# Attention with bucket masks and a mixture-of-experts step: one PSUM bank for the attention products, kd on GpSimd, most of R on VectorE, another order

## The chip, the cores and the metric

The kernel runs on one core of a Trainium2 chip. Its engines run side by side, each with its own queue of instructions, which it takes in order: TensorE (PE in the profile, its weight loads PEld), VectorE (DVE), ScalarE (ACT), GpSimd (POOL), and SyncE (SP), whose queue here issues nearly all DMAs. Semaphores tie them together. The metric is the device time of one execution in microseconds.

## The reference, cut to what matters

There are 4 batches of 8 heads, 768 tokens and 64 columns a head: 32 heads in all.

```python
q_bucket, k_bucket = hash_of(q, proj), hash_of(k, proj)      # 6 sign bits each
mask = q_bucket[:, :, :, None] == k_bucket[:, :, None, :]
scores = scale * np.matmul(q, k.transpose(0, 1, 3, 2))
scores = np.where(mask, scores, -1000000000.0)
scores = scores - np.max(scores, axis=-1, keepdims=True)
attn = np.exp(scores)
attn = attn / (np.sum(attn, axis=-1, keepdims=True) + 1e-09)
return np.matmul(attn, v)
```

A row without any key in its bucket has all its scores at the same large negative number, so its result is the mean of all values. The heads' results, side by side, are 512 columns wide per token. In each batch a gate then scores the 768 tokens, the best 128 pass through an expert (512 to 1024 columns, ReLU, back to 512), and the expert's result, times a sigmoid of the score, is added to these tokens.

## The kernel before

**Precision.** float32 operands are split into a high and a low part, and products are summed from the parts. `A` holds the high parts of q and k in rows 32 to 95, the signs of the hash bits in rows 0 to 5, and in row 96 the row maxima; `Bt` the cross parts. The signs put the mask into the scores: each differing bit lowers a score by a large amount.

**Per head**, the steps are these.

- Preparation: `load_x` brings q and k, `split_xh` (ScalarE) and `split_xl` (VectorE, line 167) split them, and `place_a`, `place_signs`, `place_b` move the parts into `A` and `Bt` by DMAs on SP's queue. For each pair of heads `load_v`, `split_vh`, `split_vl` make `V`: 64 high columns, a column of ones (times 16), 64 low columns.
- Maxima: `k_diff` (line 241, VectorE) subtracts the second half of the keys from the first. For each of six query tiles, `max_unit` (line 251) makes two 384-column products in two of the three `mx` banks, `max_relu` (line 258, ScalarE) takes the relu of one and `max_red` (line 265, VectorE) adds the other and takes the maximum over the row, since max(a, b) = relu(a - b) + b. `max_fin` (line 272) rounds the six columns, and `max_row` moves them into row 96 of `A`.
- Scores: nine units of 512 columns. `st_unit` (lines 283 and 287) makes two matmuls for each piece of a unit in a bank of `pst`, `st_exp` (lines 300 and 302, ScalarE) takes the exponential into `P`, in float32.
- R: the high half of the bits of `P` is read as a bfloat16; `r_chunk` (line 313) subtracts it from `P` and writes the rest as a float16. There are six chunks of 128 keys a head; `pool_r` says which of them GpSimd makes (four and five by turns; three and two in the last two heads), VectorE makes the others.
- Products: `av` (lines 326 and 330) takes 36 pairs of key chunk and query tile in four parts of nine. For each pair, the high part of `P` times all 129 columns of `V`, and R times the first 65. The six query tiles' sums lie in two banks of PSUM, 129 columns each: 64, the sum of the weights, and 64 from the low columns.
- Evacuation: `evac` (line 337, ScalarE) copies both banks to SBUF, `join` (line 345, GpSimd; VectorE in the last head) adds the two groups of 64 columns, `unmatched` (line 350) finds the rows whose sum is zero, `recip` and `recip2` (lines 357 and 363) make 1 / (sum + 1e-9), `norm` (line 371) multiplies into `x`, the batch's result, and `fix` (line 379) puts the mean of the values in the rows found. The means come from `load_vt` (v transposed, a load of its own), `sum_v` (line 213, ScalarE), `mean_v` (line 219, PE) and `mean_evac` (line 227, ScalarE).
- `score` (line 391, VectorE) makes the gate's scores from `x`.

**Per batch** `choose` writes `x` to the output on SP's queue, sends the scores to every partition, ranks the tokens on VectorE and gathers the chosen ones; `expert` does the rest. The experts' weights are split by `load_w` (line 415, GpSimd) in the first heads.

**The order** is written out by hand: each step is given a time in units, of which a head has nine, from the table `T` and `AVS`; all steps are emitted in the order of these times, and each engine runs its own in that order. The units count from `s0 = 9 * h`, the first unit of the head's scores; `b = s0 - 14` is the base of its maxima, `a0 = s0 + 6` that of its products. A pool with n buffers makes the tile that comes n later wait for the last reader.

PSUM's eight banks: three for `mx`, two for the scores, two for the products, one for the experts.

Of the kernel before, what the change touches and what calls it, by code (L numbers as in the profile page):

```python
# [11 lines left out]
F32 = mybir.dt.float32  # L12
# [3 lines left out]
I32 = mybir.dt.int32  # L16
# [18 lines left out]
PB = (3, 2)  # L35
XHB = 2
XLB = 2
AVS = ((0, 9, 1.34), (9, 18, 3.3), (18, 27, 5.62), (27, 36, 6.48))
# when an engine's part of the work is put in line, in units
T = dict(  # L40
    loadx=-34.22, hash=-5.69, hash2=2.32, sign=1.42, xh=-8.42, xl=-0.57, pa=-5.69, ps=0.26, loadv=-13.95,
    vh=-7.97, vl=-2.67, mean=4.21, loadt=-1.38, sumv=4.41, meane=0.56, exp=0.51, max=-0.24, kd=-1, mb=1.2,
    copy=0.71, red=2.2, fold=2.07, foldd=2.37, fin=0.81, unm=0.2, row=1.19, rp=2.6, rd=5.05, ev=0.72, rc=1.85,
    rc2=0.3, norm=0.95, fix=1.28, sc=2.97, scd=0.95, join=1.2, m1=-18.04, m2=-7.82, y1=1.01, sc3=0.3, f0=1.67,
    f1=1, f2=1.62, l0=0.84, l1=0.5, l2=1.32, l3=2.62, lw=-0.65, lw1=6.42, lw2=3.62, mo=0.38, ym=1, fold0=3.65,
# [26 lines left out]
def body(ctx, tc, qk, v, vt, pj, wg, w1, w2, cst, out):  # L72
# [131 lines left out]
    def load_vt(pr):  # L204
        t = sb.tile([P, S], F32, tag="V", name=f"VT{pr}", bufs=1)
        nc.sync.dma_start(t, vt[pr])
        st["VT", pr] = t

    def sum_v(pr):
        # the sums of the values over all tokens, one per partition  # L210
        sv = sb.tile([P, 1], F32, tag="sv", name=f"sv{pr}", bufs=2)
        jk = sb.tile([P, S], BF16, tag="jv", name=f"jv{pr}", bufs=1)
        nc.scalar.activation(jk, st["VT", pr], AF.Copy, accum_out=sv)
        st["sv", pr] = sv

    def mean_v(pr):
        # and in every partition
        mp = pmax.tile([P, 512], F32, tag="mx", name=f"mp{pr}")
        nc.tensor.matmul(
            mp[:, : 2 * D], st["sv", pr].broadcast_to([P, P]), ident, start=True, stop=True  # L220
        )
        st["mp", pr] = mp[:, : 2 * D].rearrange("p (h d) -> p h d", h=2)

    def mean_evac(pr):
        o = st["mp", pr]
        mv = sb.tile([P, 2, D], F32, tag="mv", name=f"mv{pr}", bufs=2)
        nc.scalar.activation(mv, o, AF.Copy, scale=1.0 / S)
        st["mv", pr] = mv

# [7 lines left out]
    # the row maxima: max(a, b) = relu(a - b) + b over the two halves of the keys  # L237
    def k_diff(h):
        a = A[h % NA]
        kd = sb.tile([96, 384], F32R, tag="kd", name=f"kd{h}", bufs=1)  # L240
        nc.vector.tensor_tensor(
# [28 lines left out]
    def max_fin(h):  # L270
        m = sb.tile([P, NC], F32R, tag="m", name=f"m{h}", bufs=2)
        nc.vector.tensor_copy(m, st["mA", h])
        st["m", h] = m
# [42 lines left out]
    def av(h, i0, i1):  # L316
        # (key chunk, query tile) pairs i0 to i1 of the 36
        vv, hh = V[h // 2 % NV], h % 2
        if i0 == 0:
            st["O", h] = pav.tile([P, 2, 512], F32, tag="av", name=f"av{h}")  # L320
        o = st["O", h][:, :, : 3 * (2 * D + 1)].rearrange("p e (t d) -> p e t d", t=3)
        for i in range(i0, i1):
            c, t = divmod(i, NC)
            e, j = divmod(t, 3)
            hi = hi_view(st["P", h, c // 2], c % 2)[:, t * P : (t + 1) * P]
            nc.tensor.matmul(  # L326
                o[:, e, j], hi, vv[:, c, hh], start=(c == 0 and j == 0), stop=False,
                skip_group_check=True,
            )
            nc.tensor.matmul(  # L330
                o[:, e, j, 0 : D + 1], st["R", h, c][:, t * P : (t + 1) * P],
                vv[:, c, hh, 0 : D + 1], start=False, stop=(c == NC - 1), skip_group_check=True,
            )

    def evac(h):
        o = sb.tile([P, NC, 2 * D + 1], F32, tag="o", name=f"o{h}", bufs=2)
        nc.scalar.copy(  # L337
            o.rearrange("p (e t) d -> p e (t d)", e=2), st["O", h][:, :, : 3 * (2 * D + 1)]
        )
        st["o", h] = o  # L340

    def join(h):
        o = st["o", h]
        eng = nc.gpsimd if h < NH - 1 else nc.vector
        eng.tensor_tensor(o[:, :, 0:D], o[:, :, 0:D], o[:, :, D + 1 :], op=ALU.add)  # L345

    def unmatched(h):
        # a row with a key in its bucket has a sum of about one at least
        ind = sb.tile([P, NC], F32, tag="ind", name=f"ind{h}", bufs=2)
        nc.vector.tensor_scalar(  # L350
            ind.unsqueeze(2), st["o", h][:, :, D : D + 1], VS * 1e-30, None, op0=ALU.is_le
        )
        st["ind", h] = ind

    def recip(h):
        rc = sb.tile([P, NC], F32, tag="rc", name=f"rc{h}", bufs=2)
        nc.vector.tensor_scalar(
            rc.unsqueeze(2), st["o", h][:, :, D : D + 1], VS * 1e-9, None, op0=ALU.add
        )
        st["rc", h] = rc  # L360

    def recip2(h):
        nc.vector.reciprocal(st["rc", h], st["rc", h])

    def norm(h):
# [4 lines left out]
        o, rc = st["o", h], st["rc", h]  # L370
# [4 lines left out]
    def fix(h):  # L375
        # rows without a key in their bucket: the mean of all values
        b, hh = divmod(h, H)
        x = st["x", b][:, :, hh * D : (hh + 1) * D]
        nc.vector.copy_predicated(
            x, st["ind", h].bitcast(I32).unsqueeze(2).broadcast_to([P, NC, D]),  # L380
            st["mv", h // 2][:, h % 2].unsqueeze(1).broadcast_to([P, NC, D]),
        )
# [36 lines left out]
    # the generators yield how many units to let pass  # L419
    def choose(b):  # L420
# [7 lines left out]
        # every partition gets all the scores, by way of DRAM  # L428
# [6 lines left out]
        # rank of a token: how many have a larger score, or an equal one and come earlier  # L435
# [49 lines left out]
    def gather(b, idx, xe):  # L485
        # the chosen tokens come back from the output, which holds the attention's result
# [6 lines left out]
    def expert(b, tags):  # L493
        """The expert's steps on the chosen tokens; tags: where its tiles lie."""
# [116 lines left out]
    def apply_expert(b):  # L611
        # one bank, step after step, beside the attention of later heads
# [29 lines left out]
    def apply_expert_fast(b, tags, bank, bank2):  # L642
        # two banks in turn: TensorE goes on while the other one is read
# [36 lines left out]
    def rank_last(b):  # L680
        # the last batch: its scores reach every partition by way of TensorE
# [62 lines left out]
        # keeps the array's clock up while the gather runs  # L744
# [4 lines left out]
    def moe(b):  # L749
# [8 lines left out]
        if b == 2:  # L758
            # the end of the program has room on TensorE
# [134 lines left out]
```

## Time and profile before

| | us |
|---|---|
| runs: median, lowest, highest | 581.71, 572.57, 596.73 |
| span of the profiled execution | 578.2 |
| mean granted TensorE clock | 0.900 |

The profile is of one execution. Its page gives each engine's busy time, and its groups put together instructions of the same line, with count, busy time, mean duration in ns, and the idle time of the engine just before them with what ended it. A row that gives three numbers with slashes has the shortest, the median and the longest duration in ns. A row of waits has the total, the number of waits and, where it stands, the longest. A row of the timeline has start and duration in us. A matmul's duration runs from its start until its last result, and several are under way at once, so that the distance between starts tells how long one holds up the next. The row of stretches gives each engine's busy time and the number of instructions, then the granted clock, the share of the DMA engines and GB/s.

### The profile page before, as it was taken

What the parts mean: (1) busy time and instruction counts of PE and PEld (TensorE: products, weight loads), DVE (VectorE), ACT (ScalarE), POOL (GpSimd) and SP (SyncE); (2) the same over time, 40 slices, a digit from 0 to 9 for tenths busy, and PEclk for the clock granted to TensorE, in tenths of its full rate; (3) what the DMA queues carried; (4) which work ended last, traced back from release to release, by engine and by line L of the source; (5) the groups of instructions that cost most, each with busy time, mean ns of one, the idle gap of its engine ahead of it and who ended that gap; (6) DMA issues with size and microseconds to landing.
All of it is one profiled execution on the core that took longest, in us unless ns stands there. A gap on an engine that the chain in (4) does not pass through costs nothing. (4 is left out here: it accounts for less than half of the span.)

```text
span 578.2 us, 11402 instructions
## 1 busy us (share of the span) xinstructions
PE 488.4 (84%) x4044; PEld 389.0 (67%) x4044; DVE 464.1 (80%) x981; ACT 348.7 (60%) x663; POOL 315.3 (55%) x221
## 2 busy tenths in 40 slices
PE   5798889798968778999976889889885789899796
PEld 1577777587747667687845778578764678777453
DVE  4668798978986998987885999878995998967731
ACT  2587777587846457677734657458763657674312
POOL 7076686759673656737533545448563464735310
PEclk9599889989988779999988778779997887999998
DMA  6896476356767348255564717364678424220300
GB/s 198 240 257 164 129 188 174 101 165 169 204 120 220 110 112 223 70 136 143 149 192 97 184 31 199 97 165 124 186 197 131 117 53 129 63 56 2 128 19 36
DMA packets 38920, 79.22 MB, mean 137 GB/s; under 512 B 12240, under 2 KB 12368, under 8 KB 38864
## 3 DMA queue, kind: packets, MB, share of 16 engines
q1 hardware_dynamic: 37968, 76.37, 49.9%
q0 software_dynamic: 896, 2.14, 1.1%
q8 instruction: 32, 0.52, 0.4%
q14 instruction: 24, 0.20, 0.1%
HBM read 32.07 MB, written 7.35 MB: 68 GB/s over the span
## 5 line engine op out<-in xcount | busy, mean ns | idle before, releaser
L313 POOL TENSOR_TENSOR R<-P 128x768 f16<-128x768 f32 x140 | 238.7, 1720 | 195.4 <-ACT P L302 173.5
L283 PE MATMUL st<-A 97*128 97x256 f32 (+1 forms) x384 | 143.3, 383 | 16.6 <-DMA A<-m 16.3
L265 DVE CUSTOM_DVE_ANT_0 mj<-mx,me 128x384 bf16<-128x384 f32 x192 | 105.4, 549 | 59.6 <-PE mx L251 41.4
L258 ACT ACTIVATE me<-mx 128x384 f32<-128x384 f32 x192 | 94.4, 492 | 87.5 <-PE mx L251 43.4
L300 ACT ACTIVATE P<-st 128x512 f32<-128x512 f32 x192 | 115.4, 601 | 40.3 <-PE st L287 38.9
L287 PE MATMUL st<-B 128*128 128x256 f32 (+1 forms) x384 | 137.6, 367 | 0.0
L326 PE MATMUL av<-V,P 128*128 128x129 f16 x1152 | 130.4, 232 | 0.0
L326 PEld LDWEIGHTS <-P 128*128 128x128 bf16 x1152 | 109.7, 104 | 25.1 <-issue 20.4
L330 PE MATMUL av<-V,R 128*128 128x65 f16 x1152 | 125.0, 201 | 0.3 <-DVE R L313 0.3
L251 PE MATMUL mx<-A 96*128 96x384 f32 x192 | 95.4, 497 | 32.6 <-DVE mA L265 28.0
L251 PE MATMUL mx<-kd,A 96*128 96x384 f32 x192 | 94.5, 492 | 22.2 <-DVE mA L265 15.7
L330 PEld LDWEIGHTS <-R 128*128 128x128 f16 x1152 | 109.0, 103 | 1.3 <-DVE R L313 0.5
L283 PEld LDWEIGHTS st<-A 97*128 97x128 f32 x384 | 83.6, 218 | 20.4 <-issue 16.2
L251 PEld LDWEIGHTS mx<-A 96*128 96x128 f32 x192 | 58.7, 306 | 50.5 <-DVE mA L265 37.0
L251 PEld LDWEIGHTS mx<-kd,A 96*128 96x128 f32 x192 | 58.7, 306 | 36.2 <-DVE mA L265 20.6
L287 PEld LDWEIGHTS st<-B 128*128 128x128 f32 x384 | 81.4, 212 | 0.2
L302 ACT ACTIVATE P<-st 128x512 f32<-128x512 f32 x96 | 57.5, 599 | 39.3 <-PE st L287 38.6
L313 DVE TENSOR_TENSOR R<-P 128x768 f16<-128x768 f32 x52 | 61.8, 1190 | 1.7 <-ACT P L302 1.7
L167 DVE SCALAR_TENSOR_TENSOR XL<-X,XH 128x768 fp32r<-128x768 f32 x32 | 48.1, 1504 | 1.4 <-DMA B<-XL 1.4
L345 POOL TENSOR_TENSOR o<-o 128x384 f32<-128x384 f32 x31 | 29.7, 959 | 25.9 <-ACT o L337 25.9
L371 DVE TENSOR_TENSOR x<-o,rc 128x384 f32<-128x384 f32 x32 | 41.5, 1296 | 0.7 <-POOL o L345 0.6
L337 ACT COPY o<-av 128x774 f32<-128x774 f32 x32 | 25.8, 807 | 21.3 <-PE av L330 21.3
(108 smaller groups left out, 596.0 us busy)
## 6 DMA issues: line engine op xcount, KB each, us to landing
X<-in_qk_dram SPq DMA_DIRECT2D x32, 384.0 KB
A<-XH SPq DMA_DIRECT2D x64, 192.0 KB
B<-A SPq DMA_DIRECT2D x64, 192.0 KB
B<-XL SPq DMA_DIRECT2D x64, 192.0 KB
V<-in_v_dram SPq DMA_DIRECT2D x16, 384.0 KB
VT<-in_vt_dram SPq DMA_DIRECT2D x16, 384.0 KB
out_dram<-x SPq DMA_DIRECT2D x4, 1536.0 KB
W<-in_w_dram SPq DMA_DIRECT2D x8, 512.0 KB
```

The costliest lines, as they stand in the source:

```text
L167: nc.vector.scalar_tensor_tensor(xl, st["X", h], XS, st["XH", h].bitcast(F32), op0=ALU.mult, op1=ALU.subtract)
L251: nc.tensor.matmul(pt[:, :384], qt[:, t], a[0:96, 1, 384:768] if i else st["kd", h], start=True, stop=True)
L258: nc.scalar.activation(me, st["mx", h, t, 0][:, :384], AF.Relu)
L265: nc.vector.tensor_tensor_reduce(out=jk, in0=st["mx", h, t, 1][:, :384], in1=st["me", h, t], op0=ALU.add, op1=ALU.max, scale=1.0, scalar=- ...
L283: nc.tensor.matmul(pt[:, o : o + n], a[:, 1, c * P : (c + 1) * P], a[:, 0, q0 : q0 + n], start=True, stop=False,)
L287: nc.tensor.matmul(pt[:, o : o + n], bt[:, 1, c * P : (c + 1) * P], bt[:, 0, q0 : q0 + n], start=False, stop=True,)
L300: nc.scalar.activation(pp[:, r, 0:512], pt, AF.Exp, scale=ES)
L302: nc.scalar.activation(pp[:, :, 512:768], pt.rearrange("p (a b) -> p a b", a=2), AF.Exp, scale=ES)
L313: eng.tensor_tensor(t, pp[:, r, :], hi_view(pp, r), op=ALU.subtract)
L326: nc.tensor.matmul(o[:, e, j], hi, vv[:, c, hh], start=(c == 0 and j == 0), stop=False, skip_group_check=True,)
L330: nc.tensor.matmul(o[:, e, j, 0 : D + 1], st["R", h, c][:, t * P : (t + 1) * P], vv[:, c, hh, 0 : D + 1], start=False, stop=(c == NC - 1), ...
L371: nc.vector.tensor_tensor(x, o[:, :, 0:D], rc.unsqueeze(2).broadcast_to([P, NC, D]), op=ALU.mult)
```

## The change

- The six tiles of products lie in one bank, 66 columns each (`OW`). The low columns of `V` are added onto the same 64 columns: each pair takes three matmuls of 65, 64 and 65 columns in place of two. The banks that come free go one to the scores (`PB` is 3 and 3).
- Each head's bank is opened by one more matmul, of 396 columns: `zs` times `W`, where `W` holds the sums of the values and of the weights over all keys, times 2^-60, as a high and a low part. So every key gets a tiny extra weight, and a row without a key in its bucket comes out as the mean. `sum_v` makes the sums from `V` by twelve matmuls for each pair of heads, in an `mx` bank; `sum_hi` (ScalarE) and `sum_lo` (VectorE) split them. The load of v's transpose, its sum, the means, the indicator and the predicated copy go.
- `recip` and `norm` read the products' bank directly; the copy and the join go. The reciprocal has one more step.
- `max_red` writes its maxima rounded, without `max_fin`.
- `k_diff` runs on GpSimd. GpSimd makes chunks 1 and 4 of R in every head, VectorE the other four.
- The times of many steps are others.

```diff
-PB = (3, 2)
+PB = (3, 3)
-AVS = ((0, 9, 1.34), (9, 18, 3.3), (18, 27, 5.62), (27, 36, 6.48))
+AVS = ((0, 9, 0.4), (9, 18, 3.3), (18, 27, 5.62), (27, 36, 6.91))
+DS = 2.0 ** -60
+OW = D + 2
 T = dict(
-    loadx=-34.22, hash=-5.69, hash2=2.32, sign=1.42, xh=-8.42, xl=-0.57, pa=-5.69, ps=0.26, loadv=-13.95,
-    vh=-7.97, vl=-2.67, mean=4.21, loadt=-1.38, sumv=4.41, meane=0.56, exp=0.51, max=-0.24, kd=-1, mb=1.2,
-    copy=0.71, red=2.2, fold=2.07, foldd=2.37, fin=0.81, unm=0.2, row=1.19, rp=2.6, rd=5.05, ev=0.72, rc=1.85,
-    rc2=0.3, norm=0.95, fix=1.28, sc=2.97, scd=0.95, join=1.2, m1=-18.04, m2=-7.82, y1=1.01, sc3=0.3, f0=1.67,
-    f1=1, f2=1.62, l0=0.84, l1=0.5, l2=1.32, l3=2.62, lw=-0.65, lw1=6.42, lw2=3.62, mo=0.38, ym=1, fold0=3.65,
+    loadx=-34.22, hash=-5.69, hash2=5.15, sign=1.42, xh=-7.24, xl=-0.57, pa=-5.69, ps=0.26, loadv=-13.95,
+    vh=-6.64, vl=-2.67, sumv=2.85, sumh=0.5, suml=4.53, exp=0.51, max=-0.24, kd=-1.41, mb=1.2,
+    copy=0.68, red=1.21, row=0.82, rp=2.6, rd=3.03, rc=0.47, norm=0.5, sc=2.0, scd=0.95,
+    m1=-17.79, m2=-8.2, y1=1.01, sc3=0.3, f0=5.6, f1=0.77, f2=1.98, l0=1.28, l1=2.34,
+    l2=1.09, l3=3.3, lw=-0.65, lw1=2.81, lw2=3.62, mo=0.38, ym=1,
 )
-POOL_R2 = (0, 1, 2, 3, 5)
-POOL_R = (1, 2, 4, 5)
-LAST_R = {30: (1, 3, 5), 31: (1, 4)}
+POOL_R = (1, 4)
...
+    ones16 = cp.tile([P, P], F16, name="ones16")
+    zs = cp.tile([33, P], F32R, name="zs")
+    W = [cp.tile([33, 2, OW], F32R, name=f"W{i}") for i in range(2)]
+    nc.gpsimd.memset(ones16, 1.0)
+    nc.gpsimd.memset(zs[0:32].bitcast(F32), 0.0)
+    nc.gpsimd.memset(zs[0:1].bitcast(F32), 1.0)
+    nc.gpsimd.memset(zs[32:33].bitcast(F32), 1.0)
+    for w in W:
+        nc.gpsimd.memset(w.bitcast(F32), 0.0)
...
     def sum_v(pr):
+        sp = pmax.tile([P, 512], F32, tag="mx", name=f"sp{pr}")
+        o, vv = sp[:, : 2 * OW].rearrange("p (h d) -> p h d", h=2), V[pr % NV]
+        for c in range(NC):
+            nc.tensor.matmul(
+                o[:, :, 0 : D + 1], ones16, vv[:, c, :, 0 : D + 1], start=(c == 0), stop=False,
+                skip_group_check=True,
+            )
+            nc.tensor.matmul(
+                o[:, :, 0:D], ones16, vv[:, c, :, D + 1 :], start=False, stop=(c == NC - 1),
+                skip_group_check=True,
+            )
+        st["sp", pr] = o
+
+    def sum_hi(pr):
+        nc.scalar.activation(
+            W[pr % 2][:, :, 0 : D + 1], st["sp", pr][0:33, :, 0 : D + 1], AF.Copy, scale=DS
+        )
+
+    def sum_lo(pr):
+        w = W[pr % 2][32:33, :, 0 : D + 1]
+        nc.vector.scalar_tensor_tensor(
+            w, st["sp", pr][32:33, :, 0 : D + 1], DS, w.bitcast(F32), op0=ALU.mult, op1=ALU.subtract
+        )
...
     def k_diff(h):
-        nc.vector.tensor_tensor(
+        nc.gpsimd.tensor_tensor(
...
     def av(h, i0, i1):
-            st["O", h] = pav.tile([P, 2, 512], F32, tag="av", name=f"av{h}")
+            o = st["Ob", h] = pav.tile([P, 512], F32, tag="av", name=f"av{h}")
+            st["O", h] = o[:, : NC * OW].rearrange("p (t d) -> p t d", t=NC)
+
+            nc.tensor.matmul(
+                st["O", h], zs, W[h // 2 % 2][:, hh].unsqueeze(1).broadcast_to([33, NC, OW]),
+                start=True, stop=False, skip_group_check=True,
+            )
...
+            for l, n, v0 in ((hi, D + 1, 0), (hi, D, D + 1), (lo, D + 1, 0)):
+                nc.tensor.matmul(
+                    o[:, t, 0:n], l, vv[:, c, hh, v0 : v0 + n], start=False,
+                    stop=last and l is lo, skip_group_check=True,
+                )
...
     def recip(h):
+        s = st["O", h][:, :, D : D + 1]
         rc = sb.tile([P, NC], F32, tag="rc", name=f"rc{h}", bufs=2)
+        nc.vector.tensor_scalar(rc.unsqueeze(2), s, VS, 1e-9, op0=ALU.min, op1=ALU.mult)
+        nc.vector.tensor_tensor(rc.unsqueeze(2), s, rc.unsqueeze(2), op=ALU.add)
+        nc.vector.reciprocal(rc, rc)
         st["rc", h] = rc
...
-            at(s0 + T["loadt"], load_vt, h // 2)
-            at(s0 + T["loadt"] + T["sumv"], sum_v, h // 2)
-            at(s0 + T["mean"], mean_v, h // 2)
-            at(s0 + T["mean"] + T["meane"], mean_evac, h // 2)
+            at(s0 + T["sumv"], sum_v, h // 2)
+            at(s0 + T["sumv"] + T["sumh"], sum_hi, h // 2)
+            at(s0 + T["sumv"] + T["suml"], sum_lo, h // 2)
...
         f = b + 7.5 + T["max"] + T["red"]
-        at(f + T["fin"], max_fin, h)
-        at(f + T["fin"] + T["row"], max_row, h)
+        at(f + T["row"], max_row, h)
...
-        at(a1 + T["ev"], evac, h)
-        at(a1 + T["join"], join, h)
         at(a1 + T["rc"], recip, h)
-        at(a1 + T["rc"] + T["unm"], unmatched, h)
-        at(a1 + T["rc"] + T["rc2"], recip2, h)
-        at(a1 + T["rc"] + T["rc2"] + T["norm"], norm, h)
-        a2 = a1 + T["rc"] + T["rc2"] + T["norm"] + T["fix"]
-        at(a2, fix, h)
+        a2 = a1 + T["rc"] + T["norm"]
+        at(a2, norm, h)
```

`a1` is the time of the head's last part of products, and `a2` that of its last step of normalisation, from which the gate's scores and the batch's write are counted.

More of the change, by code (lines that the diff above doesn't have):

```diff
@@ L48 @@
 FIRST = ((0, (0,)), (1, (0,)), (0, (1,)), (1, (1,)), (0, (2, 3)), (1, (2, 3)))
-POOL_R2 = (0, 1, 2, 3, 5)
-POOL_R = (1, 2, 4, 5)
-LAST_R = {30: (1, 3, 5), 31: (1, 4)}
+POOL_R = (1, 4)
 POOL_EQ = (2, 3, 5)
-def pool_r(h):
-    return LAST_R.get(h, (POOL_R, POOL_R2)[h % 2])
 def consts():
@@ L71, in body @@
 @with_exitstack
-def body(ctx, tc, qk, v, vt, pj, wg, w1, w2, cst, out):
+def body(ctx, tc, qk, v, pj, wg, w1, w2, cst, out):
     nc = tc.nc
@@ L202, in split_vl @@
         )
[L204 to L207, printed above, removed]
     def sum_v(pr):
[L211 to L220, printed above, removed]
-        )
[L222 to L228, printed above, removed]
+        sp = pmax.tile([P, 512], F32, tag="mx", name=f"sp{pr}")
[13 more added lines that the diff above has]
+            W[pr % 2][:, :, 0 : D + 1], st["sp", pr][0:33, :, 0 : D + 1], AF.Copy, scale=DS
+        )
+    def sum_lo(pr):
[3 more added lines that the diff above has]
+        )
     def unit_cols(u):
@@ L262, in max_red @@
         if t == 0:
-            st["mA", h] = sb.tile([P, NC], F32, tag="mA", name=f"mA{h}", bufs=1)
+            st["m", h] = sb.tile([P, NC], F32R, tag="m", name=f"m{h}", bufs=2)
         jk = sb.tile([P, 384], BF16, tag="jks", name=f"mj{h}_{t}", bufs=1)
@@ L266, in max_red @@
             out=jk, in0=st["mx", h, t, 1][:, :384], in1=st["me", h, t], op0=ALU.add, op1=ALU.max,
-            scale=1.0, scalar=-0.25, accum_out=st["mA", h][:, t : t + 1],
+            scale=1.0, scalar=-0.25, accum_out=st["m", h][:, t : t + 1],
         )
[L270 to L273, printed above, removed]
     def max_row(h):
@@ L311, in r_chunk @@
         t = sb.tile([P, S], F16, tag="R", name=f"R{h}_{c}", bufs=6)
-        eng = nc.gpsimd if c in pool_r(h) else nc.vector
+        eng = nc.gpsimd if c in POOL_R else nc.vector
         eng.tensor_tensor(t, pp[:, r, :], hi_view(pp, r), op=ALU.subtract)
@@ L319, in av @@
         if i0 == 0:
-            st["O", h] = pav.tile([P, 2, 512], F32, tag="av", name=f"av{h}")
-        o = st["O", h][:, :, : 3 * (2 * D + 1)].rearrange("p e (t d) -> p e t d", t=3)
+            o = st["Ob", h] = pav.tile([P, 512], F32, tag="av", name=f"av{h}")
[4 more added lines that the diff above has]
+            )
@@ L322, in av @@
+        o = st["O", h]
         for i in range(i0, i1):
             c, t = divmod(i, NC)
-            e, j = divmod(t, 3)
             hi = hi_view(st["P", h, c // 2], c % 2)[:, t * P : (t + 1) * P]
[L326 to L353, printed above, removed]
+            lo = st["R", h, c][:, t * P : (t + 1) * P]
@@ L355, in recip @@
+            last = c == NC - 1
+            for l, n, v0 in ((hi, D + 1, 0), (hi, D, D + 1), (lo, D + 1, 0)):
[3 more added lines that the diff above has]
+                )
     def recip(h):
+        s = st["O", h][:, :, D : D + 1]
         rc = sb.tile([P, NC], F32, tag="rc", name=f"rc{h}", bufs=2)
-        nc.vector.tensor_scalar(
-            rc.unsqueeze(2), st["o", h][:, :, D : D + 1], VS * 1e-9, None, op0=ALU.add
-        )
+        nc.vector.tensor_scalar(rc.unsqueeze(2), s, VS, 1e-9, op0=ALU.min, op1=ALU.mult)
@@ L360, in recip @@
+        nc.vector.tensor_tensor(rc.unsqueeze(2), s, rc.unsqueeze(2), op=ALU.add)
+        nc.vector.reciprocal(rc, rc)
         st["rc", h] = rc
-    def recip2(h):
-        nc.vector.reciprocal(st["rc", h], st["rc", h])
     def norm(h):
@@ L369, in norm @@
         x = st["x", b][:, :, hh * D : (hh + 1) * D]
-        o, rc = st["o", h], st["rc", h]
+        o, rc = st["O", h], st["rc", h]
         nc.vector.tensor_tensor(
             x, o[:, :, 0:D], rc.unsqueeze(2).broadcast_to([P, NC, D]), op=ALU.mult
-        )
[L375 to L381, printed above, removed]
         )
@@ L791, in body @@
         at(max(x0 + T["pa"], free), place_a, h)
-        at(max(x0 + T["ps"], free), place_signs, h)
+        at(max(x0 + max(T["ps"], T["hash"] + T["hash2"] + T["sign"] + 0.1), free), place_signs, h)
         at(s0 - 9 * NBB + 9, place_b, h)
@@ L811, in body @@
         f = b + 7.5 + T["max"] + T["red"]
-        at(f + T["fin"], max_fin, h)
-        at(f + T["fin"] + T["row"], max_row, h)
+        at(f + T["row"], max_row, h)
         for c in range(NC):
-            at(s0 + 3 * (c // 2) + (T["rp"] if c in pool_r(h) else T["rd"]) + (c % 2) * 0.1, r_chunk, h, c)
+            at(s0 + 3 * (c // 2) + (T["rp"] if c in POOL_R else T["rd"]) + (c % 2) * 0.1, r_chunk, h, c)
         a0 = s0 + 3 + AVLAG
@@ L872 @@
     ).reshape(NH // 2, P, NC, 2, D)
-    vt = np.ascontiguousarray(v.transpose(0, 1, 3, 2)).reshape(NH // 2, P, S)
     pj = np.zeros((P, 32), f)
@@ L878 @@
     arrays = {
-        "qk": qk, "v": vv, "vt": vt, "pj": pj, "wg": wg,
+        "qk": qk, "v": vv, "pj": pj, "wg": wg,
         "w1": np.ascontiguousarray(moe_w1), "w2": np.ascontiguousarray(moe_w2),
```

## The prediction

> **What bounds the kernel now.** I read the page first, for the busy shares, then the busy time by stretches, because start and end have other limits than the middle, then the waits, then the groups by line.
>
> ```profile
> span 578.2 us, 11402 instructions
> PE 488.4 (84%) x4044; PEld 389.0 (67%) x4044; DVE 464.1 (80%) x981; ACT 348.7 (60%) x663; POOL 315.3 (55%) x221
> core 0: us, PE busy (x) PEld busy (x) DVE busy (x) ACT busy (x) POOL busy (x), PEclk, DMA share, GB/s
> 60.00:540.00 480.00, 411.40 (x3583) 337.70 (x3582) 409.96 (x855) 303.40 (x579) 275.21 (x178) 0.90 0.51 133
>   DVE mA L265: 101.3, 81
> PE st L283 <- DMA A<-m: 16.3, 6, 6.3
> L337 ACT COPY o<-av x32: 805/807/817, 44.0 to 535.4; 128x774 f32<-128x774 f32 x32
> ```
>
> In the middle 480 us PE and VectorE (DVE) are both busy 85%. They aren't equal, though. A matmul's time here is its passage through the array, and many overlap, so a busy PE still has room. The fifth line is what line 251's matmuls and their weight loads waited for: 101.3 us in 81 waits for VectorE's maximum to free a bank. So in the middle VectorE sets the pace more often than PE. The last line gives the pace: 31 heads between 44.0 and 535.4 us, 15.85 us each, so one of the nine units that the order is written in is 1.76 us. The sixth is a DMA: six waits, 16.3 us, for the row of maxima to land.
>
> Why is VectorE slow? Compare its means with its medians.
>
> ```profile
> L313 POOL TENSOR_TENSOR R<-P 128x768 f16<-128x768 f32 x140 | 238.7, 1720 | 195.4 <-ACT P L302 173.5
> L265 DVE CUSTOM_DVE_ANT_0 mj<-mx,me 128x384 bf16<-128x384 f32 x192 | 105.4, 549 | 59.6 <-PE mx L251 41.4
> L313 DVE TENSOR_TENSOR R<-P 128x768 f16<-128x768 f32 x52 | 61.8, 1190 | 1.7 <-ACT P L302 1.7
> L167 DVE SCALAR_TENSOR_TENSOR XL<-X,XH 128x768 fp32r<-128x768 f32 x32 | 48.1, 1504 | 1.4 <-DMA B<-XL 1.4
> L371 DVE TENSOR_TENSOR x<-o,rc 128x384 f32<-128x384 f32 x32 | 41.5, 1296 | 0.7 <-POOL o L345 0.6
> L379 DVE COPY_PREDICATED x<-ind,mv 128x384 f32<-128x384 int32 x32 | 31.5, 986 | 0.1
> L241 DVE TENSOR_TENSOR kd<-A 96x384 fp32r<-96x384 f32 x32 | 29.8, 932 | 4.9 <-PE mx L251 3.4 <-issue 0.4 <-DMA A<-XH 0.2
> L391 DVE CUSTOM_DVE_ANT_0 jks<-x,wgt,sc 128x256 bf16<-128x256 f32 (+1 forms) x24 | 21.8, 907 | 0.7
> L391 DVE CUSTOM_DVE_ANT_0 jks<-x,wgt 128x256 bf16<-128x256 f32 x24 | 19.3, 803 | 0.3
> L350 DVE TENSOR_SCALAR ind<-o 128x6 f32<-128x6 f32 x32 | 13.3, 416 | 0.0
> L357 DVE TENSOR_SCALAR rc<-o 128x6 f32<-128x6 f32 x32 | 9.8, 307 | 3.5 <-ACT o L337 3.3
> L272 DVE CAST m<-mA 128x6 fp32r<-128x6 f32 x32 | 9.6, 301 | 0.2
> L469 DVE COPY rank<-rp 128x6 f32<-128x6 f32 x3 | 0.5, 153 | 0.0
> L345 POOL TENSOR_TENSOR o<-o 128x384 f32<-128x384 f32 x31 | 29.7, 959 | 25.9 <-ACT o L337 25.9
> L415 POOL TENSOR_TENSOR w2l<-W,w2h 128x512 bf16<-128x512 f32 x8 | 12.4, 1546 | 0.0
> L415 POOL TENSOR_TENSOR w1l<-W,w1h 128x512 bf16<-128x512 f32 x8 | 11.5, 1432 | 1.2 <-ACT w1h L413 1.2
> L313 DVE TENSOR_TENSOR R<-P x52: 935/954/2216, 30.9 to 530.8; 128x768 f16<-128x768 f32 x52
> L167 DVE SCALAR_TENSOR_TENSOR XL<-X,XH x32: 944/954/3262, 11.2 to 486.2; 128x768 fp32r<-128x768 f32 x32
> L371 DVE TENSOR_TENSOR x<-o,rc x32: 544/1815/1826, 49.6 to 538.7; 128x384 f32<-128x384 f32 x32
> L391 DVE CUSTOM_DVE_ANT_0 jks<-x,wgt x24: 410/424/1685, 98.6 to 502.7; 128x256 bf16<-128x256 f32 x24
> ```
>
> The same multiply of line 371 takes 0.544 or 1.8 us. What reads SBUF stretches two- to threefold at times; line 265, which reads the same 384 columns, one operand from PSUM, stays at 0.549. GpSimd works on SBUF 292.3 us (238.7 + 29.7 + 12.4 + 11.5) beside it, and I take that as the cause. The Trainium skill, "SBUF — State Buffer", section "Who interferes with whom", says so: a VectorE instruction with two SBUF inputs contends with a GpSimd one that reads SBUF, one with a single SBUF input does not. The 0.549 beside the 1.8 us agrees.
>
> **VectorE, part by part.** Removed: the predicated copy 31.5, kd (to GpSimd) 29.8, the indicator 13.3, the cast of the maxima 9.6: -84.2 us. The normalisation now reads PSUM; with line 265's 0.549 it costs 32 x 0.549 = 17.6 in place of 41.5: -23.9. The first step of the reciprocal becomes two steps on 6 columns; at line 469's 0.153 (6 columns from PSUM), 64 x 0.153 = 9.8, as line 357 now: 0. New is the low part of the value sums, 16 times on 130 columns: between 0.153 and 0.549 each, I take 0.35, the middle, since its size lies between: +5.6.
>
> R, the largest term: GpSimd keeps 2 of 6 chunks a head, so 64 in all, and VectorE gets 128 in place of 52. GpSimd's SBUF time becomes 64 x 1.720 + 32 kd x 0.959 (line 345, 384 columns) + 23.9 of weights = 164.7, 56% of 292.3. R's excess over its clear time, 1.190 - 0.954 = 0.236, I scale with it: 0.954 + 0.13 = 1.086; 128 x 1.086 - 61.8 = +77.2. The excess of line 167 (48.1 - 32 x 0.954 = 17.6) and of line 391 (41.1 - 48 x 0.424 = 20.7) loses 44%: -16.8.
>
> Sum: -84.2 - 23.9 + 5.6 + 77.2 - 16.8 = -42.1. VectorE is busy 410 of 480 us in the middle, and in the rest something else ends the wait, so I put 0.854 of it on the path: **-36.0**. Bounds: all stretching gone, 128 x 0.954, gives -83.7, on the path -71.5. R always as in its slower half ((61.8 - 26 x 0.954) / 26 = 1.42), no relief elsewhere, sums at 0.549: +20.7, on the path +17.7.
>
> **PE.** Each pair of products (129 and 65 columns) becomes three of 65, 64 and 65, each with its own weight load; 36 a head, 1152 in all.
>
> ```profile
> 305.75 0.23 PE L326 MATMUL av<-V,P 128*128 128x129 f16 x1
> 305.81 0.20 PE L330 MATMUL av<-V,R 128*128 128x65 f16 x1
> 305.84 0.22 PE L326 MATMUL av<-V,P 128*128 128x129 f16 x1
> 313.70 0.30 PE L326 MATMUL av<-V,P 128*128 128x129 f16 x1
> 313.79 0.26 PE L330 MATMUL av<-V,R 128*128 128x65 f16 x1
> 313.86 0.30 PE L326 MATMUL av<-V,P 128*128 128x129 f16 x1
> 316.32 0.34 PE L251 MATMUL mx<-A 96*128 96x384 f32 x1
> 316.50 0.28 PE L283 MATMUL st<-A 97*128 97x256 f32 x1
> L219 PE MATMUL mp<-cs,sv 128*128 128x128 f32 x32 | 6.2, 276 | 0.0
> ```
>
> Starts tell what a matmul holds up: 0.06 us for 129 columns, 0.03 for 65, so a pair is 0.09 and three are 0.09: nothing at full clock. After a stall (313.70) a pair is 0.16 and a 65-column step 0.07, three 0.21: +0.05. The granted clock is 0.90; if the low state is half, it holds a fifth of the time: 1152 x 0.05 x 0.2 = +11.5. The value sums are 12 matmuls of 128 or 130 columns for each of 16 pairs: 192 x 0.06 = 11.5. The matmul that opens the bank has 396 columns, as line 251's 384: 32 x 0.18 = 5.8. The removed means were 6.2 of busy time; I take off 3. Sum +25.8. PE has room, but it waits and is waited for in turn; between 0.15 (VectorE's idle share) and all of it I put a third on the path: **+8.6**. Bounds: 11.1 at 0.15, +1.7; all triples at low clock and all on the path, 11.5 + 5.8 + 57.6, +74.9.
>
> **The one bank.** Nothing copies the products out any more, so the next head's first product waits until VectorE has normalised. In the order the last products are put at 12.91 units, the reciprocal at 13.38, the normalisation at 13.88, the next head's first at 15.40: 2.5 units, 4.4 us, for a chain of about 1 us. I count 0; if VectorE's queue is late, each head pays (rival). ACT loses the copy, the value sums and their evacuation; at 60% it isn't the bound: 0. A third bank for the scores takes the freed one, and lets PE run ahead: counted with the 0 too, from no gain to a part of VectorE's idle time.
>
> **Queues and order.** On SP 16 loads of v's transpose go. The write of a batch is put 16.26 units after its last head's start in place of 20.21, and the row of maxima 4.71 units before its head's scores in place of 2.54: 2.17 units, 3.8 us, more to land behind a write. The waits at line 283 are 16.3 in six, 6.3 the longest; between 0 and all I take **-12**, since most are shorter than 3.8 plus the earlier write. The sums hold one of three maxima banks for 4.5 units of every 18; an added wait of 101.3 / 81 = 1.25 a pair would be 20 us, none is 0; the maximum is now taken right behind its matmul, so I take **+2**. On GpSimd kd stands just ahead of R's chunk 1, and waits for PE to have read the kd before; the products need that chunk 3.7 units later, which hides it. For kd at the start, behind the added memsets, which line 241's 0.932 bounds: **+0.5**.
>
> **The end.** There the last head's chain is bare.
>
> ```profile
> 537.37 0.55 DVE L345 TENSOR_TENSOR o<-o 128x384 f32<-128x384 f32 x1
> 539.30 0.59 DVE L379 COPY_PREDICATED x<-ind,mv 128x384 f32<-128x384 int32 x1
> ```
>
> From 537.37 to 539.89 are 2.52 us, and 0.81 of copy ahead; left are 3 x 0.153 + 0.55 = 1.01: **-2.3**.
>
> **Sum:** 578.2 - 36.0 + 8.6 - 12 + 2 + 0.5 - 2.3 = 539.0 us of span. The median of the runs, 581.7, lies 3.5 above this execution's span; with it 542.5, rounded to 542.
>
> **The rivals.**
> - More gain: the stretching all but goes, the waits for the row go, and PE's part hides: 578.2 - 71.5 + 1.7 - 16.3 - 2.3 + 3.5 = 493. For it: GpSimd's load nearly halves. Against: kd and R's chunk 1 lie just where VectorE starts its own chunk 0.
> - R gets no faster on VectorE: it meets GpSimd's chunks each time and takes 1.42. Then VectorE's sum is 42.7 less good (128 x 1.42 against 139.0), about 0: 542 + 36.5 = 579.
> - The one bank is a new wait: if each of 31 heads costs PE one mean wait of 1.25, +38.8: 581. It starts where VectorE is over 3 us late at the reciprocal. Against: it is placed well ahead.
> - PE sets the pace (the other side): it is the busiest engine on the page, the change adds only to it, and VectorE's gain is then idle time. 578.2 + 25.8 - 12 - 2.3 + 3.5 = 593, with all triples at 0.21 642, the middle 618. It decides once PE's additions pass its 68.6 idle us in the middle: if a triple costs 0.05 more at every clock. Against: 0.03 us a step at full clock. The Trainium skill, "TensorE: Matmul & The Clock Gate", section "Back-to-back issue gap", sets about 81 ns for each pair of weight load and matmul at 128 columns; by that a third one adds 0.081 x 1152 = 93 us, an estimate, and this rival would hold. The trace here shows 0.03 and 0.06.
>
> **How the numbers follow.** Forecast 0.55 (518 to 566), more gain 0.17, R unrelieved 0.10, the bank 0.08, PE 0.10. The time is the forecast's, 542. From 500 to 582 leaves out the lower half of the second case and nearly all of the last, together two in ten. By 2%, about what a measurement of this kernel can tell from no change: faster 0.75 (the first two and a part of the third), within 0.15, slower 0.10.
>
> **What would show it.** Right: VectorE's busy time near 422, GpSimd's near 185, the normalisation at 0.55, R on VectorE near 1.09, line 283's wait for the row nearly gone, products 0.03 us apart. Wrong: R at 1.4; PE waiting for the normalisation ahead of a head's first product; products 0.07 apart through the middle; maxima that wait while the sums hold their bank; a first score that still waits for the row.

## The result, and the profile after

| | before | after |
|---|---|---|
| median, us (beside each other) | 579.16 | 559.58 |
| lowest, highest | 572.57, 596.73 | 556.32, 563.33 |
| span of the profiled execution | 578.2 | 561.6 |

The ratio is 0.971, with a 95% interval of 0.963 to 0.979: faster by about 17 us. Some executions of a kernel come out over 1.5% longer than its fastest (596.73 is one): medians, lowest and highest include them, while the ratios and intervals, here and below, as a rule leave them out. The forecast of 542 against 581.7 was a ratio of 0.932; the way was right, the size more than double.

From the page, the view of stretches and the waits of the changed kernel; the last line, again from the page, is each engine's share of the chain of work that ended last:

```profile
span 561.6 us, 13874 instructions
PE 504.1 (90%) x5388; PEld 391.8 (70%) x5388; DVE 456.7 (81%) x976; ACT 317.1 (56%) x599; POOL 182.9 (33%) x152
60.00:540.00 480.00, 440.29 (x4973) 349.65 (x4969) 410.93 (x889) 279.51 (x531) 152.53 (x112) 0.96 0.49 129
PEld mx L257 <- DVE m L271: 29.0, 35, 1.8
PE mx L257 <- DVE m L271: 17.9, 24, 1.6
PE st L284 <- DMA A<-m: 1.9, 2, 1.1
PE 50%; DVE 19%; issue 10%; DMA 8%; ACT 4%; POOL 1%; SPq 0%; POOLq 0%; DVEq 0%; ACTq 0%
```

GpSimd's busy time is 183 us, where about 185 was forecast, and PE's waits for the row of maxima have gone from 16.3 to 1.9 us. But VectorE (DVE) is busy 456.7 us, 7.4 less than before, where 42 less was forecast. And PE, busy 411 of the middle 480 us before, is now busy 440. On the chain PE holds half of the span and VectorE 19%, some 107 of its 457 busy us. The page of the kernel before follows its chain for only 2% of the span, so there is nothing to set beside it.

PEld stands for the weight loads, which have a queue of their own. Where waits of PE and PEld are added below, as the prediction did, they lie partly side by side, so that such a sum is more than the time that PE stood.

The groups by line, and all durations of R (shortest, median, longest, in ns):

```profile
L314 DVE TENSOR_TENSOR R<-P 128x768 f16<-128x768 f32 x128 | 171.6, 1361 | 23.1 <-ACT P L303 21.8
L314 POOL TENSOR_TENSOR R<-P 128x768 f16<-128x768 f32 x64 | 106.5, 1664 | 237.0 <-ACT P L303 237.0
L247 POOL TENSOR_TENSOR kd<-A 96x384 fp32r<-96x384 f32 x32 | 33.8, 1056 | 80.5 <-PE mx L257 73.2
L173 DVE SCALAR_TENSOR_TENSOR XL<-X,XH 128x768 fp32r<-128x768 f32 x32 | 31.5, 985 | 0.8 <-DMA B<-XL 0.7
L355 DVE TENSOR_TENSOR x<-av,rc 128x384 f32<-128x384 f32 x32 | 17.8, 557 | 1.2 <-DVE rc L346 0.2
L314 DVE TENSOR_TENSOR R<-P x128: 941/954/4267, 30.1 to 519.0; 128x768 f16<-128x768 f32 x128
```

The normalisation reads PSUM and takes 0.557 us, no longer stretched; line 173 has come down from 1.504 to 0.985. R alone has not: its median is 0.954 as before, its mean 1.361. So few instructions carry a large excess. Sorted by chunk, it is chunk 0: it lasts over 2.2 us in 21 of 32 heads, and it holds 46.9 of the 52.1 us by which the 128 chunks together exceed 0.954 each. The timeline shows one of them, first VectorE's, then GpSimd's at that time:

```profile
255.78 2.92 DVE L314 TENSOR_TENSOR R<-P 128x768 f16<-128x768 f32 x1 [0.52 <-ACT P L303]
255.45 1.00 POOL L247 TENSOR_TENSOR kd<-A 96x384 fp32r<-96x384 f32 x1 [2.05 <-PE mx L257]
256.41 1.47 POOL L314 TENSOR_TENSOR R<-P 128x768 f16<-128x768 f32 x1
```

VectorE's chunk 0 and GpSimd's chunk 1 become ready with the same exponential, and kd stands just ahead of chunk 1. Chunk 0 starts at 255.78, finds kd under way, and ends at 258.70: 0.82 us after GpSimd is through with both, near its own 0.95. So it is hardly slowed, it waits for nearly the whole of GpSimd's work. In 19 of the 21 heads kd and chunk 1 both run in that time, in the last two heads, which have no kd left to make, chunk 1 alone. The Trainium skill, "SBUF — State Buffer", section "Who interferes with whom", calls the ports that VectorE shares with GpSimd an exclusive lock and says that issue order decides who blocks. The trace agrees on the lock, with 2.10 us of waiting; on the order it agrees for kd but not for R, which started at 256.41, 0.63 us after chunk 0, and still ran first.

### The profile page after: what moved, and what is told of

Read it like the earlier page. It is cut to its first block, busy times and chain, and to the rows that moved or that the text cites. A ratio compares the mean times of both kernels' runs of the same rounds, so it can differ in the third digit from the quotient of the medians.

```text
span 561.6 us, 13874 instructions
## 1 busy us (share of the span) xinstructions
PE 504.1 (90%) x5388; PEld 391.8 (70%) x5388; DVE 456.7 (81%) x976; ACT 317.1 (56%) x599; POOL 182.9 (33%) x152
## 4 chain that ended last, share of the span: by engine, by line
PE 50%; DVE 19%; issue 10%; DMA 8%; ACT 4%; POOL 1%; SPq 0%; POOLq 0%; DVEq 0%; ACTq 0%
PE av L335 13%; PE mx L257 12%; PE st L284 8%; PE st L288 7%; DVE R L314 6%; DVE mj L271 4%; PE yp L550 3%; DMA W<-in_w_dram 2%; PE mh L515 2%; DMA A<-m 2%; DMA scores<-sc 2%; DVE jks L366 2%; ACT P L303 2%; DVE XL L173 1%; PE av L324 1%
## 5 line engine op out<-in xcount | busy, mean ns | idle before, releaser
L314 DVE TENSOR_TENSOR R<-P 128x768 f16<-128x768 f32 x128 | 171.6, 1361 | 23.1 <-ACT P L303 21.8
L314 POOL TENSOR_TENSOR R<-P 128x768 f16<-128x768 f32 x64 | 106.5, 1664 | 237.0 <-ACT P L303 237.0
L288 PE MATMUL st<-B 128*128 128x256 f32 (+1 forms) x384 | 132.1, 354 | 0.0
L335 PEld LDWEIGHTS <-P 128*128 128x128 bf16 x2304 | 114.6, 99 | 22.6 <-issue 16.2
L335 PE MATMUL av<-V,P 128*128 128x65 f16 (+1 forms) x2304 | 129.4, 197 | 0.8 <-issue 0.7
L284 PEld LDWEIGHTS st<-A 97*128 97x128 f32 x384 | 79.1, 206 | 3.2 <-DMA A<-m 2.4
L247 POOL TENSOR_TENSOR kd<-A 96x384 fp32r<-96x384 f32 x32 | 33.8, 1056 | 80.5 <-PE mx L257 73.2
L173 DVE SCALAR_TENSOR_TENSOR XL<-X,XH 128x768 fp32r<-128x768 f32 x32 | 31.5, 985 | 0.8 <-DMA B<-XL 0.7
L168 ACT ACTIVATE XH<-X 128x768 fp32r<-128x768 f32 x32 | 26.8, 837 | 2.9 <-DMA X<-in_qk_dram 2.7
L149 PE MATMUL hp<-X,pjt 128*32 128x384 f32 x128 | 21.0, 548 | 7.3 <-DMA X<-in_qk_dram 7.3
```

What stands on the lines that cost most here:

```text
L168: nc.scalar.activation(xh, st["X", h], AF.Copy, scale=XS)
L173: nc.vector.scalar_tensor_tensor(xl, st["X", h], XS, st["XH", h].bitcast(F32), op0=ALU.mult, op1=ALU.subtract)
L247: nc.gpsimd.tensor_tensor(kd, a[0:96, 1, 0:384].bitcast(F32), a[0:96, 1, 384:768].bitcast(F32), op=ALU.subtract)
L284: nc.tensor.matmul(pt[:, o : o + n], a[:, 1, c * P : (c + 1) * P], a[:, 0, q0 : q0 + n], start=True, stop=False,)
L288: nc.tensor.matmul(pt[:, o : o + n], bt[:, 1, c * P : (c + 1) * P], bt[:, 0, q0 : q0 + n], start=False, stop=True,)
L314: eng.tensor_tensor(t, pp[:, r, :], hi_view(pp, r), op=ALU.subtract)
```

## The experiments

Two theories stood against each other at first: V, that VectorE's stretched instructions hold the changed kernel back, and P, that PE does by now. All times are medians, and each is compared with runs of the kernel before beside it, which took 576 to 579 us; the changed kernel's ratio is 0.971. The changed kernel's own four runs went from 563.3 us at a granted clock of 0.943 to 556.3 at 0.955, so a few us between variants of it tell nothing.

**Chunk 0 later.** The line is the one that orders `r_chunk`.

```diff
-... (T["rp"] if c in POOL_R else T["rd"]) ...
+... (T["rp"] if c in POOL_R else T["rd"] + (1.95 if c == 0 else 0)) ...
```

> The changed kernel with VectorE's chunk 0 of R put 1.95 units later, behind the normalisation, so that it no longer starts together with GpSimd's chunk 1. Theory V (VectorE's stretched instructions stand on the path): the mean of R on VectorE falls from 1.361 us to about 1.0, VectorE's busy time from 457 to about 412 us, and the time by 25 to 40 us, to 520 to 535. Theory P (PE sets the pace of the changed kernel): VectorE's busy time falls just as much, and the time stays within 8 us of 560.

563.4 us, ratio 0.977 (0.971 to 0.984). From its page, its durations of R and its waits:

```profile
PE 510.0 (91%) x5388; PEld 398.2 (71%) x5388; DVE 409.3 (73%) x976; ACT 316.0 (56%) x599; POOL 178.6 (32%) x152
L314 DVE TENSOR_TENSOR R<-P x128: 943/953/2053, 33.6 to 518.5; 128x768 f16<-128x768 f32 x128
PEld L335 <- DVE R L314: 12.1, 22, 3.8
PE av L335 <- DVE R L314: 8.0, 8, 3.7
```

The stretching is nearly gone, the longest R is 2.1 in place of 4.3 us, and VectorE is busy 47 us less. The time is no better. The products now wait for chunk 0, which comes late, but PE stood only 8.0 us for it, 20 with its weight loads, not 47.

**No low part of v.**

```diff
-            for l, n, v0 in ((hi, D + 1, 0), (hi, D, D + 1), (lo, D + 1, 0)):
+            for l, n, v0 in ((hi, D + 1, 0), (lo, D + 1, 0)):
```

> The changed kernel without the 64-column matmuls of the low part of v, so 1152 matmuls and weight loads fewer; it leaves that part of the products out. They hold up the next one for 0.035 us each, 40 us in all. Theory V: a third of it or less shows, 13 us or less. Theory P: 30 to 40 us.

560.0 us, ratio 0.972 (0.968 to 0.976): no gain either. Its page, its waits and the row with its clock:

```profile
PE 489.5 (88%) x4236; PEld 369.3 (66%) x4236; DVE 466.4 (84%) x976; ACT 317.1 (57%) x599; POOL 177.4 (32%) x152
PEld mx L257 <- DVE m L271: 36.0, 40, 2.4
PE mx L257 <- DVE m L271: 23.3, 29, 1.7
core 0: 557.5 us, clock 0.905
```

So P doesn't hold as it stood either. With 1152 matmuls fewer, PE and its loads wait 12.4 us more for VectorE's maximum (59.3 against 46.9), VectorE is busy 10 us more, for R is stretched more (its mean is 1.492), and PE's granted clock is 0.905 in place of 0.943. What PE gets through sooner it loses by waiting, and by running slower. How much PE's time would be worth at an even clock, this run doesn't tell.

**Write and row late.**

```diff
-    copy=0.68, red=1.21, row=0.82, ...
+    copy=0.68, red=1.21, row=2.99, ...
-    ... mo=0.38, ...
+    ... mo=4.33, ...
```

> The changed kernel with the row of maxima and the batch's write put back to their distances of the kernel before (2.54 and 20.21 units). If the new places are what took away the waits for the row of maxima, they come back: some 16 us of PE's waits at the scores, and 10 to 16 us of time. If the waits went for another reason (fewer loads on the queue), nothing comes back and the time stays within 4 us.

576.7 us, ratio 1.001 (0.997 to 1.005): with these two places put back, nothing of the change's gain is left. Its waits:

```profile
PEld st L284 <- DMA A<-m: 9.2, 5, 4.3
PE st L284 <- DMA A<-m: 5.8, 4, 4.0
PE av L324 <- DVE x L355: 11.2, 11, 2.4
```

The wait for the row comes back in part, and the wait for the one bank grows from 3.5 to 11.2 us. For `mo` moves not the write alone: the second half of the gate's scores, the ranking and the selection are counted from it and go along, and in three batches the scores then stand ahead of the next head's normalisation on VectorE (2.43 us of PE's idle time each).

**Chunk 5 left out.**

```diff
+            if c < NC - 1:
...
-            lo = st["R", h, c][:, t * P : (t + 1) * P]
+            lo = st["R", h, min(c, 4)][:, t * P : (t + 1) * P]
```

> The changed kernel without chunk 5 of R, which is VectorE's and lasts 1.035 us in the mean: 33 us of VectorE's time go, nothing on the other engines; the products take chunk 4's R again in its place, so a part of the sums is another. Theory V: 0.854 of it, 28 us of time. Theory P: less than 8 us.

549.2 us, ratio 0.955 (0.949 to 0.962): 9 us better than the changed kernel for 37 us of VectorE's busy time (420.0), between the theories.

**Both, and more of both.** The first two edits together:

> The first two together: chunk 0 of R 1.95 units later and no 64-column matmuls (the low part of v left out of the products). Alone neither moved the time. If TensorE and VectorE stand so close that each takes over where the other is relieved, both together give 20 to 35 us (525 to 540). If a third thing sets the pace (the queue of DMAs, ScalarE), the time stays within 6 us of 560.

552.9 us, ratio 0.962 (0.953 to 0.971): 5 us better, within the intervals, with VectorE 43 us and PE 18 us less busy, and a granted clock of 0.904. That is far from the 20 to 35 us of two engines that only take over from each other, and near the case of a third thing; which one it is, this run doesn't show. With chunk 0 late and chunk 5 left out:

> Chunk 0 of R 1.95 units later and chunk 5 left out (the products take chunk 4's again): VectorE's busy time about 375 us, 80 less than in the changed kernel. Leaving out chunk 5 alone gave 10 us. If TensorE takes over where VectorE is relieved, it is now the only one left and the time stays between 545 and 556. If VectorE's time counts with a share, 80 us give 25 or more: 535 or less.

552.6 us, ratio 0.956 (0.948 to 0.964), VectorE's busy time 374.1: the 46 us beyond the run without chunk 5 give nothing. That is the case in which TensorE takes over: VectorE is down to 68% of the span, PE at 91%. Chunk 0 at a middle place, 1.2 in place of 1.95 units:

> The changed kernel with VectorE's chunk 0 of R 1.2 units later in place of 1.95, ahead of the reciprocal. If the later place cost back what the relief gave, because the first products wait for chunk 0 (12.1 us of such waits there), an earlier one keeps the relief of VectorE (R below 1.2 us in the mean) with half of these waits, and the time is 5 to 12 us below 560. If VectorE's relief is worth nothing, within 4 us.

555.6 us, ratio 0.964 (0.955 to 0.972). Its page:

```profile
PE 495.2 (89%) x5372; PEld 388.7 (70%) x5388; DVE 421.1 (76%) x976; ACT 314.2 (57%) x599; POOL 179.0 (32%) x152
```

VectorE's 421.1 is the 422 of the prediction, and worth 4 us, within the intervals.

**The banks of the maxima.**

```diff
-PB = (3, 3)
+PB = (4, 2)
```

> The changed kernel with PSUM shared out otherwise: four banks for the maxima and two for the scores, in place of three and three. Theory L (the pace is a loop: a product of the maxima, ScalarE's relu, VectorE's maximum, and only then the bank for the product three later): PE's 46.9 us of waits for VectorE's maximum fall by half or more and the time by 8 to 20 us, less what the third bank of the scores was worth. Theory C (TensorE and VectorE are both near full, buffers matter little): within 5 us of 560.

559.5 us, ratio 0.972 (0.967 to 0.977). Its waits:

```profile
PEld mx L257 <- DVE m L271: 4.1, 10, 1.2
PE mx L257 <- DVE m L271: 0.4, 2, 0.2
PE av L324 <- DVE x L355: 11.1, 13, 1.8
PE hp L149 <- DMA X<-in_qk_dram: 11.0, 7, 4.7
```

The wait for VectorE's maximum all but goes, 4.5 in place of 46.9 us, and the time stays: theory L, of a loop through three banks, falls as the pace, unless the third bank of the scores was worth just as much. Others grow in its place: for the one bank 11.1 (3.5 in the changed kernel), for the loads of q and k 11.0 (7.3). With `PB = (2, 3)`:

> The changed kernel with two banks for the maxima in place of three, one of PSUM's eight unused. Theory L: the loop is tighter, 30 us or more on top (590 or more). Theory C: less than 15 us on top.

650.2 us, ratio 1.12 (1.11 to 1.13): three are needed, a fourth isn't. With two, the value sums leave the maxima a single bank while they hold theirs; the run doesn't tell that part from the rest. The sums' bank given back sooner, `suml=1.0` in place of 4.53, alone and with chunk 0 in the middle:

> The changed kernel with VectorE's step on the value sums 1.0 units behind the matmuls in place of 4.53, so that the sums hold one of the three banks of the maxima for a quarter of the time. The prediction put +2 us on this: 0 to 3 us less. Theory L: 4 to 10 us less.

> Chunk 0 of R 1.2 units later (555.6 alone) and the step on the value sums at 1.0 units. If both relieve different waits, their gains add: 550 to 554. If not, 555 or above.

563.4 us (558.1 to 572.8), ratio 0.970 (0.964 to 0.975), and 562.3, ratio 0.976 (0.972 to 0.980): no gain, and the second loses what chunk 0 gave.

**The kernel before, relieved.** Does VectorE's time count there?

```diff
-        at(a1 + T["rc"] + T["unm"], unmatched, h)
...
-        at(a2, fix, h)
```

> The kernel before without the indicator of unmatched rows and the predicated copy: 44.8 us of VectorE's busy time go, nothing else; rows without a key in their bucket keep zeros. If VectorE's time counts with 0.854, as the prediction had it, 38 us less (538). If another engine or another wait takes over, less than 12 us.

551.8 us, ratio 0.955 (0.947 to 0.963): 26 us less. Its page:

```profile
PE 475.9 (86%) x4044; PEld 382.1 (69%) x4044; DVE 431.2 (78%) x917; ACT 347.9 (63%) x663; POOL 312.1 (57%) x221
```

VectorE's busy time fell by 32.9 and not by 44.8, mostly because in the trace 12.4 us of those 44.8 lie over the instructions next to them, and busy time counts such time once. 26 of 32.9 is 0.79: in the kernel before VectorE does set the pace, as far as this one edit shows, which also shortens the chain behind the products.

**The write early, and what moves with it.** In the kernel before, `mo=-2.9` in place of 0.38, which moves the write and, with it, the second half of the scores, the ranking and the selection; then also `hash2=5.15`, with the signs' move behind it; then the first without the indicator and the copy:

> The kernel before with nothing changed but the batch's step that starts with the write to the output, put 3.28 units earlier, right behind the last head's result, so that on the DMA queue the write and the scores come as in the changed kernel. If the write's place made the whole gain, this kernel takes 10 to 18 us less than before (560 to 567) and its waits at line 283 for the row of maxima fall from 16 us to below 5. If the gain needs the rest of the change, it stays within 4 us of before.

> The kernel before with the early write and with the hash's second half 5.15 units behind the first in place of 2.32, as in the changed kernel. If the early write gave nothing there because its scores on VectorE kept the hash from its bank (36.0 us of such waits, 8.7 before), these waits fall below 10 us and the time to 560 to 568. If the gain needs VectorE's relief, it stays at 576 or above.

> The kernel before with the early write and without the indicator and the predicated copy; rows without a key in their bucket keep zeros. With the late write it took 551.8. If the early write needs VectorE's relief and that is all, it now gives 10 us or more: 542 or less. If it needs another part of the change (the order of the maxima, the place of the row), it costs as in the kernel before: 554 or more.

584.1 us, ratio 1.010 (1.001 to 1.019); 588.9 (582.0 to 591.8), ratio 1.023 (1.015 to 1.032), not told apart from the first; 561.2, ratio 0.975 (0.967 to 0.983), 9 us worse than with the late write. The second one's waits, and one stop of PE in its timeline:

```profile
PEld hp L143 <- DVE mA L265: 27.9, 11, 5.6
PE hp L143 <- DVE mA L265: 24.3, 8, 5.1
PE st L283 <- DMA A<-m: 2.3, 2, 1.5
PE ip L477 <- DVE sel L472: 10.0, 3, 4.0
157.27 0.48 DVE L391 CUSTOM_DVE_ANT_0 jks<-x,wgt,sc 128x256 bf16<-128x256 f32 x1
157.94 0.56 DVE L265 CUSTOM_DVE_ANT_0 mj<-mx,me 128x384 bf16<-128x384 f32 x1 [0.17 <-DVE sc L391]
158.56 1.50 PE L143 MATMUL hp<-X,pjt 128*32 128x384 f32 x6 [4.87 <-DVE mA L265]
```

The early write does end the wait for the row there, 16.3 to 2.3 us. But the hash of the next heads then waits 52.2 us for a bank that VectorE holds, 8.7 before. Most of that is due to the scores that moved along: six of them run on VectorE from 151.51 to 157.75, ahead of the maximum at 157.94 that frees the bank, and PE stands 4.87 us. It does so about as long in each of three batches, 15 of the 24.3 us. PE also stands 10.0 us in three waits of the selected tokens' products (L477) for the selection on VectorE, a wait that the kernel before doesn't have. So these runs priced the write together with steps that cost more than it gave, and the write alone was not tried. Moving the hash doesn't help (52.2 us against 36.0 without it), nor is it enough to relieve VectorE (28.8 us in the third run, and 10.0 for the selection again). In the changed kernel the wait for the selection is 1.0 us; which part of its order keeps both away was not tried. The hash's second half put back to 2.32 units in the changed kernel does no harm:

> The changed kernel with the hash's second half back at 2.32 units. If its place matters beside the early write, 8 us or more on top of 560 and more waits of the hash for VectorE's maximum. If not, within 4 us.

555.5 us, ratio 0.966 (0.959 to 0.973).

**What gained, together.** Chunk 0 in the middle and four banks for the maxima; then the hash's place too:

> The changed kernel with chunk 0 of R 1.2 units later (555.6 alone) and four banks for the maxima, two for the scores (559.5 alone). If the fourth bank takes waits away that the third one of the scores doesn't need, 545 to 552. If the waits only move, 554 or above.

> The changed kernel with chunk 0 of R 1.2 units later, four banks for the maxima and two for the scores, and the hash's second half at 2.32 units. The three gave 4, 0 and 4 us alone, the first two together 7. If the waits are different ones, 545 to 550; if they only move, 551 or above.

552.8 us, ratio 0.959 (0.952 to 0.965), and 550.6, ratio 0.953 (0.943 to 0.963): better than the kernel before, and the second some 10 us below the changed one, with intervals that just touch. The waits of the first:

```profile
PEld hp L149 <- DMA X<-in_qk_dram: 14.7, 8, 3.3
PE hp L149 <- DMA X<-in_qk_dram: 13.8, 8, 4.8
```

With the maxima and VectorE relieved, the loads of q and k come too late: 28.5 us of waits, 12.5 in the changed kernel; PE itself stands 13.8 in place of 7.3. That may be a third limit behind the two. It is read from the waits; no run took it away.

## Why the prediction was right or wrong

- **0.854 of VectorE's time on the path: the step that failed.** The prediction turned busy time saved on VectorE into time of the kernel at 0.854, the share of the middle in which VectorE was busy (410 of 480 us). In the kernel before it nearly holds: 0.79. In the changed kernel it doesn't: 36 us of busy time gave 4, 47 gave none, and the 37 of chunk 5 gave 9, a quarter. The chain of the changed kernel agrees: 107 of VectorE's 457 busy us lie on it. The run with chunk 0 in the middle is the plain test, for it has VectorE's forecast busy time with all the rest of the change in place: 555.6 us, and not 542.
- **What took over** is shown in part. The prediction's own PE terms filled the room that PE had, 69 us of idle time in the middle, 40 after, and on the chain PE holds half of the span. But with matmuls taken away as well there were only 5 us, at a lower clock of PE. So PE is the likeliest engine to have taken over, and what stands behind both, the clock, the loads or the order, stays open.
- **R, the term that was mis-sized.** The prediction scaled R's excess with GpSimd's total SBUF time, to 1.086 us, +77.2. It was 1.361, +109.8, and these 32.6 us are nearly all that VectorE's sum missed: -42.1 + 32.6 = -9.5, measured -7.4. Not how long GpSimd works decides, but whether kd and chunk 1 run while chunk 0 is due: chunk 0 and chunk 1 wait for the same exponential, and kd stands ahead of chunk 1. The prediction named this meeting, as a reason against more gain, and gave it no term. The rival "R gets no faster" (1.42) was nearer in R's mean, but for another reason: three chunks of four are nearly clear, one waits. Moving chunk 0 alone brought VectorE to the forecast busy time or below, and the time by at most 4 us, so a right R would not have given 542 either.
- **PE.** A product holds up the next for 0.03 us at full clock, three in 0.09, and each brings its own weight load, as forecast:

```profile
365.93 0.24 PE L335 MATMUL av<-V,P 128*128 128x65 f16 x2
366.01 0.19 PE L335 MATMUL av<-V,R 128*128 128x65 f16 x1
366.04 0.22 PE L335 MATMUL av<-V,P 128*128 128x65 f16 x2
366.10 0.19 PE L335 MATMUL av<-V,R 128*128 128x65 f16 x1
366.13 0.22 PE L335 MATMUL av<-V,P 128*128 128x65 f16 x2
370.18 0.42 PE L324 MATMUL av<-W,zs 33*128 33x396 f32 x1
370.53 0.24 PE L335 MATMUL av<-V,P 128*128 128x65 f16 x2
```

  From 366.04 to 366.13 is one triple, 0.09; a row marked x2 is two matmuls. The opening matmul holds up the next for 0.35, not 0.18: +5 us more than its term. The rival that PE alone sets the pace (618) is refuted as a forecast by the time; the run without the low part speaks against it too, as far as its lower clock allows.
- **The write and the row.** -12 was right in size: the wait fell by 14.4 us. Putting both places back cost 17, so these places carried the gain: with them late the rest of the change nets to nothing. The 17 are not the row's wait alone, though, for the scores and the ranking move with the write and added 7.7 us of waits for the one bank. Which of the two places counts was not told apart. In the kernel before the early write, with what moves along, gave nothing; the row's place was not tried there.
- **The one bank:** 3.5 us of waits in all; counting 0 was right. **The sums' bank:** giving it back sooner changed nothing, so +2 can't be told from 0. **ACT and GpSimd:** on the chain they hold 4% and 1% of the span, so counting 0 was near, though PE and its loads wait 27.7 us for ScalarE's relu.
- **The sum with VectorE's measured 7.4** in place of 42.1 is 578.2 - 6.3 + 8.6 - 12 + 2 + 0.5 - 2.3 = 568.7 us of span, 7 more than the 561.6 measured. That looks as if R's excess were most of the miss, but it is luck: the sum prices R with the same 0.854 that the runs above refute. What the other terms were worth one by one, no run took apart.

## What to carry to other kernels

Contention between two engines goes by instructions, not by totals: look for pairs that are released by the same event, and price the one that waits with the whole of what runs ahead of it. A share of the path that is read from one kernel need not hold in the next (here 0.79, then a quarter or less): add the change's own load to the next engine first, and ask what that engine leaves of the gain. The place of a DMA and of the steps counted from it can be worth as much as all arithmetic saved, and its worth depends on the order around it. Before an edit is read as the price of one step, look what else moves with it.

## What the runs showed of the hardware that was not expected

- VectorE's instruction with two SBUF operands waited through two GpSimd instructions that followed each other, kd and R, and ran only then: 2.92 us in place of 0.95.
- Taking 1152 matmuls out of PE's stream brought its granted clock from 0.943 to 0.905, and from 0.928 to 0.904 with chunk 0 late.
- A matmul of 396 float32r columns with 33 rows holds up the next for 0.35 us, one of 384 with 96 rows for 0.18. Why was not tried.
